# Attention's denominators gathered from SBUF to SBUF on ScalarE's queue, with their VectorE steps placed behind the newest subtraction

## The chip, the core and the metric

The kernel runs on one core of a Trainium2 chip. A core has five engines, each of which works through its own list of instructions in order: TensorE (PE in the profile) multiplies matrices, VectorE (DVE), ScalarE (ACT) and GpSimd (POOL) work element by element, and SyncE (SP) here only issues transfers. TensorE adds up its products in PSUM banks, the other tiles lie in SBUF, inputs and results in DRAM, and transfers (DMA) move data between them. An instruction that needs another engine's result waits on a semaphore, and everything behind it in its engine's list waits too. The metric is the device time of one execution in microseconds (us), smaller being better.

## The reference

Three blocks follow each other, all in fp32:

```
# attention: q, k, v are (4 batches, 8 heads, 576 tokens, 64), w_phi is (64, 128)
phi(x) = [exp(p - m), exp(-(p - m))],  p = x @ w_phi,  m = max |p| over the 128 features
kv  = sum over s of phi(k)[s, f] * v[s, d];   z = sum over s of phi(k)[s, f]
x   = (phi(q) @ kv) / (phi(q) @ z + 1e-6)            # -> 2304 tokens x 512
# ELU block: w_in (512, 2048), w_out (2048, 512)
x1  = elu(x @ w_in) @ w_out
# four experts: w1 (512, 1024), w2 (1024, 512), p = probs normalised per token
out = sum over e of p[:, e] * (relu(x1 @ w1[e]) @ w2[e])
```

## The kernel before

The work is written as Python generators; a scheduler that follows a simulated timeline then fixes each engine's list when the program is built. What was written earlier has the higher priority, and an instruction that looks ready in that timeline may be placed ahead of earlier ones that do not.

**Attention** runs over 16 pairs of heads, four to a batch, called p0 to p15 here. `pair(i)` is one generator. It projects K and Q with `w_phi` on TensorE (`md` holds the last 64 tokens of both, L205; K and Q are L188). VectorE takes the largest magnitude of each token and subtracts it (`guard`, L194 and L195), which gives `md`, `kp0`, `kp1`, `qd0` and `qd1`. ScalarE takes the exponentials of K (L198, L199). TensorE transposes Q (L234, L272), multiplies K's features with V (L227, L228) and forms the numerators (`num`, L307). V carries a column of ones, so that each head's denominator falls out as one row of its 128-row result. ScalarE copies the results to `nd0` and `nd1` (L309), 128 partitions by 576 tokens each.

The **denominators' path** is the end of `pair`. SyncE writes the two denominator rows to DRAM (`dscr`, L316), reads them back as a tile of 128 partitions by 9 (`dn`, L319), VectorE adds 1e-6 and takes the reciprocal (L321, L322), SyncE writes that to DRAM (`rscr`, L323) and reads it back broadcast over 64 partitions a head (`rb`, L327), and VectorE multiplies `nd` by it into `xf` (L331, two halves). `put_x` splits `xf` into `xh` and `xl` (ScalarE L291, GpSimd L294) and stores it.

`attention()` keeps about three pairs going: a new one starts every five rounds, and a round advances each pair by one `yield`. So while pair i is at its products, pair i+1 is in the middle and pair i+2 at its K projection.

**The ELU block** runs over nine tiles of 256 tokens and four units each. `l1` multiplies `x` by `w_in` in three products (L493 to L495), `g` is made by ScalarE (L501, L502) and VectorE (L504), split into `gh` and `gl`, and `l2` multiplies by `w_out` (L522 to L524). Between matmuls it calls `slot()`, which advances attention and the weights a little. A tile of 256 tokens needs all four pairs of its batch, so the tiles that start a new batch are written behind as many attention steps as that takes.

**The weights** of this block come as 64-bit words and are converted in 64 pieces (`convert64`): a load (L103), two ScalarE operations (L111, L112), four VectorE operations on `pcs`, `top` and `w` (L114 to L117), and two to three GpSimd and ScalarE operations. `weight_stream` keeps `CVB` = 4 of them going.

**After attention** come the upper half of the ELU block (L613 to L615, L692 to L694) and the experts (L613 to L615, L715 to L717).

SyncE's list holds the loads of K, Q, V and weights and the denominators' transfers of all pairs, in one order.

Of the kernel before, what the change touches and what calls it, by code (L numbers as in the profile page):

```python
# [8 lines left out]
F32 = mybir.dt.float32  # L9
F32R = mybir.dt.float32r  # L10
U32 = mybir.dt.uint32
I64 = mybir.dt.int64
ACTF = mybir.ActivationFunctionType
ALU = mybir.AluOpType
# [3 lines left out]
B, H, S, D, FEAT = 4, 8, 576, 64, 128  # L18
NT, DM, DFF, E, F2 = 2304, 512, 2048, 4, 1024
P = 128  # L20
KD = DM // P
NP = H // 2
# [22 lines left out]
RATE = 1.4  # L45
WRATE = 2
CVB = 4
TAIL = 2
ATE = 6
WSLOW = 2.5  # L50
# [7 lines left out]
CVW = 256  # L58
# [6 lines left out]
def attn_elu_moe_kernel(ctx: ExitStack, tc: tile.TileContext, kq_in, vv, w_phi, w_in, w_out, probs, w1, w2, out):  # L65
    nc = tc.nc
    V, A, G, PE, SP = nc.vector, nc.scalar, nc.gpsimd, nc.tensor, nc.sync
# [9 lines left out]
    dram = ctx.enter_context(tc.tile_pool(name="dram", bufs=1, space=bass.MemoryType.DRAM))  # L77
# [2 lines left out]
    x1fin = [[dram.tile([P, KD, TC], F32, name=f"x1fin{g}_{s}") for s in range(2)] for g in range(NG)]  # L80
    yscr = [dram.tile([P, DM], F32, name=f"yscr{r}") for r in range(NT // P)]
    xvd = [[dram.tile([P, 2, 2, TC], F32, name=f"xvd{g}_{k}") for k in range(7)] for g in range(NG)]
    dscr, rscr = ([dram.tile([2, S], F32, name=f"{n}{i}") for i in range(B * NP)] for n in ("den", "rec"))
    x1scr = [dram.tile([P, KD, TS], F32, name=f"x1scr{t}") for t in range(NTS)]
    ring = pool("ring", RING)
    pst = ExitStack()
# [4 lines left out]
    cv = pool("cv", CVB, stack=right, side="right")  # L91
# [7 lines left out]
        V.tensor_tensor(out=pr, in0=pr, in1=prr.to_broadcast([P, NT // P, E]), op=ALU.mult)  # L99

    def convert64(dst, src, adder):
        st = cv.tile([P, CVW], I64, tag="w64", name="w64")
        SP.dma_start(st, src)  # L103
        yield
        words = st.bitcast(U32).rearrange("p (n two) -> p n two", two=2)
        lo, hi = words[:, :, 0], words[:, :, 1]
        top = cv.tile([P, CVW], U32, tag="top", name="top")
        unit[0] += 1
        ps = pcs[:, unit[0] % 2]
        bits = ps.bitcast(U32)  # L110
        A.activation(ps, f32(hi), ACTF.Abs)  # L111
        A.activation(f32(lo), lo, ACTF.Copy, scale=2.0 ** -52)  # L112
        yield
        V.tensor_scalar(out=ps, in0=ps, scalar1=MINF, scalar2=MAXF, op0=ALU.max, op1=ALU.min)  # L114
        V.tensor_scalar(out=bits, in0=bits, scalar1=3, scalar2=0x3FFFFFF8, op0=ALU.logical_shift_left, op1=ALU.bitwise_and)
        V.scalar_tensor_tensor(out=top, in0=hi, scalar=0xC0000000, in1=bits, op0=ALU.bitwise_and, op1=ALU.bitwise_or)
        V.tensor_scalar(out=hi, in0=top, scalar1=0xFF800000, scalar2=None, op0=ALU.bitwise_and)  # L117
        yield
        G.tensor_tensor(out=f32(lo), in0=f32(lo), in1=f32(hi), op=ALU.mult)
        yield  # L120
        adder.tensor_tensor(out=f32(top), in0=f32(top), in1=f32(lo), op=ALU.add)
        if dst.dtype == F32:
            yield
            SP.dma_start(dst, f32(top))
            return
        A.activation(dst[:, 0], f32(top), ACTF.Copy)
        yield
        G.tensor_tensor(out=dst[:, 1], in0=f32(top), in1=f32(dst[:, 0]), op=ALU.subtract)
# [6 lines left out]
    a1 = pool("a1", stack=att)  # L135
# [35 lines left out]
    loaded = {0: load(0)}  # L171

    def blocks(t, n):
        return t[:, :n * P].rearrange("p (n f) -> p n f", f=P)

    def pair(i):
        b, p = divmod(i, NP)
        kq, v = loaded.pop(i)
# [12 lines left out]
        def guard(dst, ps, n):  # L191
            src = blocks(ps, n)
            mx = a1.tile([P, n, 1], F32, tag=f"mx{n}", name="mx", bufs=2)
            V.tensor_reduce(out=mx[:, :, 0], in_=src, op=ALU.max, axis=AX.X, apply_absolute_value=True)  # L194
            V.tensor_tensor(out=dst, in0=src, in1=mx.to_broadcast([P, n, P]), op=ALU.subtract)  # L195

        def kexp(d0, d1, src):
            A.activation(d0, src, ACTF.Exp)  # L198
# [84 lines left out]
        xf = a1.tile([P, S], F32, tag="xf", name="xf")  # L283
# [10 lines left out]
                G.tensor_tensor(out=xl[:, p, c:c + n], in0=xf[:, o:o + n], in1=f32(xh[:, p, c:c + n]), op=ALU.subtract)  # L294
                o += n

        nd = [a1.tile([P, S], F32, tag=f"nd{h}", name=f"nd{h}") for h in range(2)]

        def num(s):
            sl = slice(s * HS, (s + 1) * HS)  # L300
# [10 lines left out]
        num(0)  # L311
        yield
        num(1)
        yield
        for h in range(2):
            SP.dma_start(dscr[i][h:h + 1, :], nd[h][D - h * D:D - h * D + 1, :])  # L316
        yield
        dn = a1.tile([P, S // D], F32, tag="dn", name="dn")
        SP.dma_start(dn, dscr[i].rearrange("h (a b) -> (h a) b", b=S // D))  # L319
        yield  # L320
        V.tensor_scalar(out=dn, in0=dn, scalar1=1e-6, scalar2=None, op0=ALU.add)  # L321
        V.reciprocal(out=dn, in_=dn)  # L322
        SP.dma_start(rscr[i].rearrange("h (a b) -> (h a) b", b=S // D), dn)  # L323
        yield
        rb = a1.tile([P, S], F32, tag="rb", name="rb")
# [2 lines left out]
        yield  # L328
        for h in range(2):
            r = slice(h * D, h * D + D)  # L330
            V.tensor_tensor(out=xf[r], in0=nd[h][r], in1=rb[r], op=ALU.mult)  # L331
        put_x()

    done = [0]
# [69 lines left out]

    def weight_stream():
        todo = conversions()
        live = []
        more = True
        while more or live:
            if more and len(live) < CVB:  # L410
                g = next(todo, "end")
                if g == "end":
                    more = False
                else:
                    live.append(g)
            for _ in range(2):
                for g in list(live):
                    with tc.high_priority(offset=CVOFF):
                        ended = next(g[0], "end") == "end"
                    if ended:  # L420
                        live.remove(g)
                        nm, f, o = g[1]
                        if nm == "out" and f % 2 and o + CVW == 512:
                            ready.add(("elu", f // 2))
                    yield
            if not live:
                yield
        while wst[0] is None:
            yield
        for e in range(-1, E):  # L430
            for q in range(NQ):
                st = []
# [48 lines left out]
    class Elu:  # L481
# [4 lines left out]
        def l1(self, slot):  # L486
            xh, xl = xt[self.t]
            ph = bank((P, 2, TS))
            for j in range(2):
                w = rings["in", 2 * self.u + j]  # L490
                for kc in range(KD):
                    c = slice(kc * P, (kc + 1) * P)
                    PE.matmul(ph[:, j], w[:, 0, c], xh[:, kc], start=(kc == 0), stop=False)  # L493
                    PE.matmul(ph[:, j], w[:, 0, c], xl[:, kc], start=False, stop=False)  # L494
                    PE.matmul(ph[:, j], w[:, 1, c], xh[:, kc], start=False, stop=(kc == KD - 1))  # L495
                if j == 0:
                    slot()
            g = tmp.tile([P, 2, TS], F32, tag="g", name="g")
            self.gh = gt.tile([P, 2, TS], F32R, tag="gh", name="gh")
            self.gl = gt.tile([P, 2, TS], F32R, tag="gl", name="gl")  # L500
            A.activation(g, ph, ACTF.Relu, scale=-1.0)  # L501
            A.activation(g, g, ACTF.Exp, scale=-1.0)  # L502
            slot()
            V.scalar_tensor_tensor(out=g, in0=g, scalar=1.0, in1=ph, op0=ALU.subtract, op1=ALU.max)  # L504
            A.activation(self.gh, g, ACTF.Copy)  # L505
            (V if self.t >= GLV else G).tensor_tensor(out=self.gl, in0=g, in1=f32(self.gh), op=ALU.subtract)  # L506
            if self.t == NTS - 1:
                release(("in", 2 * self.u), ("in", 2 * self.u + 1))
# [458 lines left out]
```

## Time and profile before

| | us |
|---|---|
| median of 3 runs | 1439.79 |
| lowest, highest | 1436.64, 1442.32 |
| the profiled execution's own time | 1437.25 |
| its span, first to last instruction | 1435.2 |

| engine | busy us | share of the span |
|---|---|---|
| TensorE, matmuls | 1376.3 | 96% |
| VectorE | 690.8 | 48% |
| ScalarE | 630.4 | 44% |
| GpSimd | 418.5 | 29% |

The mean granted TensorE clock is 0.983, where 1 is 2.4 GHz and 0.5 is 1.2 GHz. The shares are means over stages that differ: up to about 400 us attention shares the engines with the ELU block, and from about 500 us on TensorE hardly pauses. In a table by stretches the columns are the stretch, its length, the busy time of PE, PEld, DVE, ACT and POOL with the number of instructions, the granted clock, the DMA engines' share and GB/s. In a timeline they are start, duration, engine, line, operation and tiles, and in brackets the idle time of that engine just before and what ended it. A table of waits gives, for each pair of waiting and awaited instruction, the total, the number of times and the longest, in us.

### The profile page before, as it was taken

The numbers are of one execution on the slowest core, as the hardware profiler recorded it, in microseconds if no ns is written. First come the engines' busy times: TensorE is split into PE (matmuls) and PEld (weight loads), VectorE is DVE, ScalarE is ACT, GpSimd is POOL, SyncE is SP. The second block draws the span as 40 slices with busy tenths as digits, with TensorE's granted clock in tenths as the row PEclk, the third lists the DMA queues.
The fourth block names the chain that finished last, engine by engine and source line by source line (L and its number), as shares of the span: only waits on it lengthen the run. The fifth ranks groups of instructions, "written<-read, shape, count | busy, mean of one in ns | idle before, by whom it ended". The sixth has DMA issues, their size and how long they took to land.

```text
span 1435.2 us, 21878 instructions
## 1 busy us (share of the span) xinstructions
PE 1376.3 (96%) x8224; PEld 1269.6 (88%) x8224; DVE 690.8 (48%) x1233; ACT 630.4 (44%) x1417; POOL 418.5 (29%) x487
## 2 busy tenths in 40 slices
PE   6789989999999899999999999999999999999998
PEld 5678879899989899999988988898988989889897
DVE  7767677544365384776334333233432335323232
ACT  5667667555545664574333433122431214322121
POOL 5547676533324420254212341001330004300000
PEclk9889989999999999999999999999999999999999
DMA  5443555322041412336433323524154361433421
GB/s 163 131 139 109 171 161 163 106 86 60 33 132 52 133 61 73 115 127 232 150 132 121 118 78 118 199 90 154 45 161 173 97 209 50 139 110 133 167 75 66
DMA packets 105594, 173.53 MB, mean 121 GB/s; under 512 B 33264, under 2 KB 50800, under 8 KB 105488
## 3 DMA queue, kind: packets, MB, share of 16 engines
q1 hardware_dynamic: 100592, 162.70, 35.0%
q10 hardware_dynamic: 4896, 9.44, 1.8%
q8 instruction: 64, 1.05, 0.3%
q14 instruction: 42, 0.34, 0.1%
HBM read 118.21 MB, written 53.89 MB: 120 GB/s over the span
## 4 chain that ended last, share of the span: by engine, by line
PE 71%; DMA 6%; DVE 3%; issue 2%; ACT 1%; POOL 1%; SPq 0%; DVEq 0%; POOLq 0%; ACTq 0%
PE bank L615 9%; PE bank L613 9%; PE bank L614 9%; PE bank L715 9%; PE bank L716 9%; PE bank L717 9%; PE bank L692 2%; PE bank L693 2%; PE bank L694 2%; PE bank L523 1%; PE bank L522 1%; PE bank L307 1%; PE bank L524 1%; PE bank L493 1%; PE bank L494 1%
## 5 line engine op out<-in xcount | busy, mean ns | idle before, releaser
L614 PE MATMUL bank<-xv,w 128*128 128x384 f32 x840 | 282.0, 336 | 0.0
L613 PE MATMUL bank<-xv,w 128*128 128x384 f32 x840 | 278.5, 336 | 3.0 <-DVE c L664 2.2
L615 PE MATMUL bank<-xv,w 128*128 128x384 f32 x840 | 277.9, 336 | 0.0
L715 PE MATMUL bank<-w,h 128*128 128x512 f32 x576 | 225.8, 395 | 2.6 <-ACT h L629 2.6
L716 PE MATMUL bank<-w,h 128*128 128x512 f32 x576 | 227.4, 395 | 0.0
L717 PE MATMUL bank<-w,h 128*128 128x512 f32 x576 | 202.9, 396 | 0.0
L455 POOL TENSOR_TENSOR w<-wst,w 128x256 fp32r<-128x256 f32 x100 | 78.1, 800 | 363.1 <-ACT w L454 348.0
L613 PEld LDWEIGHTS bank<-xv,w 128*128 128x128 f32 x840 | 157.8, 188 | 11.3 <-DVE c L664 2.5
L614 PEld LDWEIGHTS bank<-xv,w 128*128 128x128 f32 x840 | 157.8, 188 | 4.8
L615 PEld LDWEIGHTS bank<-xv,w 128*128 128x128 f32 x840 | 157.5, 188 | 0.0
L630 DVE SCALAR_TENSOR_TENSOR h<-bank,h 128x384 fp32r<-128x384 f32 x144 | 77.1, 554 | 125.5 <-ACT h L629 125.4
L629 ACT ACTIVATE h<-bank 128x384 fp32r<-128x384 f32 x144 | 66.8, 489 | 152.4 <-PE bank L615 94.7
L715 PEld LDWEIGHTS bank<-w,h 128*128 128x128 f32 x576 | 108.2, 188 | 25.6 <-ACT h L629 3.6
L716 PEld LDWEIGHTS bank<-w,h 128*128 128x128 f32 x576 | 108.3, 188 | 23.0
L717 PEld LDWEIGHTS bank<-w,h 128*128 128x128 f32 x576 | 107.2, 188 | 21.9 <-DVE h L630 1.1
L619 ACT ACTIVATE cmab<-bank 128x384 f32<-128x384 f32 x60 | 29.4, 491 | 192.3 <-PE bank L615 192.3
L564 POOL TENSOR_TENSOR xv<-xs,xv 128x768 fp32r<-128x768 f32 x24 | 46.7, 1950 | 191.2 <-ACT xv L563 182.5
L493 PE MATMUL bank<-xh,w 128*128 128x256 f32 x288 | 85.0, 295 | 0.4 <-DVE g L504 0.2
L523 PE MATMUL bank<-gl,w 128*128 128x256 f32 x288 | 81.8, 286 | 3.0 <-DVE gl L506 2.5
L627 DVE TENSOR_TENSOR c<-cmab,bank 128x384 f32<-128x384 f32 x48 | 26.6, 554 | 120.1 <-ACT cmab L619 120.1
L522 PE MATMUL bank<-gh,w 128*128 128x256 f32 x288 | 81.2, 292 | 3.0 <-ACT gh L505 3.0
L494 PE MATMUL bank<-xl,w 128*128 128x256 f32 x288 | 81.9, 284 | 0.0
(117 smaller groups left out, 2803.4 us busy)
## 6 DMA issues: line engine op xcount, KB each, us to landing
xv<-xvd SPq DMA_DIRECT2D x42, 768.0 KB
wst<-in_w SPq DMA_DIRECT2D x64, 256.0 KB
xvd<-xv SPq DMA_DIRECT2D x21, 768.0 KB
yscr<-y SPq DMA_DIRECT2D x54, 256.0 KB
y<-yscr SPq DMA_DIRECT2D x54, 256.0 KB
w<-in_w_in SPq DMA_DIRECT2D x32, 256.0 KB
w<-in_w_out SPq DMA_DIRECT2D x32, 256.0 KB
kq<-in_kq SPq DMA_DIRECT2D x16, 320.0 KB
```

The lines of the kernel that those rows point to most:

```text
L455: on[WL[v % len(WL)]].tensor_tensor(out=lo, in0=x, in1=f32(hi), op=ALU.subtract)
L493: PE.matmul(ph[:, j], w[:, 0, c], xh[:, kc], start=(kc == 0), stop=False)
L494: PE.matmul(ph[:, j], w[:, 0, c], xl[:, kc], start=False, stop=False)
L522: PE.matmul(o, w[:, 0, c], self.gh[:, j], start=start, stop=False)
L523: PE.matmul(o, w[:, 0, c], self.gl[:, j], start=False, stop=False)
L613: PE.matmul(o, hi[:, c], x[:, 0, kc], start=not more and kc == 0, stop=False, skip_group_check=more)
L614: PE.matmul(o, hi[:, c], x[:, 1, kc], start=False, stop=False, skip_group_check=more)
L615: PE.matmul(o, lo[:, c], x[:, 0, kc], start=False, stop=kc == 1, skip_group_check=more)
L630: V.scalar_tensor_tensor(out=h[:, 1], in0=c, scalar=0.0, in1=f32(h[:, 0]), op0=ALU.max, op1=ALU.subtract)
L715: PE.matmul(self.acc, h[:, 0, c], w[:, 0], start=f == 0, stop=False)
L716: PE.matmul(self.acc, h[:, 0, c], w[:, 1], start=False, stop=False)
L717: PE.matmul(self.acc, h[:, 1, c], w[:, 0], start=False, stop=f == 2 * NQ - 1)
```

## The change

It has four parts.

1. `dn` is filled directly from the denominator rows in `nd0` and `nd1`, by two transfers from SBUF to SBUF (L319 of the new kernel, 64 partitions by 9 each), issued by ScalarE. The DRAM tile `dscr`, its three transfers per pair on SyncE and two `yield`s per pair are gone.
2. The steps of VectorE on the denominators (add, reciprocal, and the two products into `xf`) may not be placed ahead of the newest subtraction written so far: `mark` holds the last L195 or L504 instruction, and `tc.issue_after` adds an edge of order, without a semaphore.
3. `nd0` and `nd1` have two buffers each.
4. `weight_stream` keeps `CVL` = 2 further pieces loaded, whose load has been issued and whose conversion has not begun.

```
-        nd = [a1.tile([P, S], F32, tag=f"nd{h}", name=f"nd{h}") for h in range(2)]
+        nd = [a1.tile([P, S], F32, tag=f"nd{h}", name=f"nd{h}", bufs=2) for h in range(2)]
...
         num(1)
-        yield
-        for h in range(2):
-            SP.dma_start(dscr[i][h:h + 1, :], nd[h][D - h * D:D - h * D + 1, :])
-        yield
         dn = a1.tile([P, S // D], F32, tag="dn", name="dn")
-        SP.dma_start(dn, dscr[i].rearrange("h (a b) -> (h a) b", b=S // D))
-        yield
-        V.tensor_scalar(out=dn, in0=dn, scalar1=1e-6, scalar2=None, op0=ALU.add)
-        V.reciprocal(out=dn, in_=dn)
+        for h in range(2):
+            A.dma_start(dn[h * D:h * D + D], nd[h][D - h * D:D - h * D + 1, :].rearrange("o (a b) -> o a b", b=S // D))
+        yield
+        with tc.issue_after(mark[0]):
+            V.tensor_scalar(out=dn, in0=dn, scalar1=1e-6, scalar2=None, op0=ALU.add)
+            V.reciprocal(out=dn, in_=dn)
...
-            V.tensor_tensor(out=xf[r], in0=nd[h][r], in1=rb[r], op=ALU.mult)
+            with tc.issue_after(mark[0]):
+                V.tensor_tensor(out=xf[r], in0=nd[h][r], in1=rb[r], op=ALU.mult)
...
-        while more or live:
-            if more and len(live) < CVB:
+        while more or loaded or live:
+            if more and len(loaded) < CVL:
                 g = next(todo, "end")
...
-                    live.append(g)
+                    next(g[0])
+                    loaded.append(g)
+            if loaded and len(live) < CVB and (len(loaded) == CVL or not more):
+                live.append(loaded.pop(0))
```

`mark[0]` is set where `guard` subtracts and where L504 of the old kernel computes `g`.

The lists of the engines, first VectorE's in the first batch. The names end in a number of their own; `nd0_585` and `nd0_595` belong to p1, and `kp0_694` and `kp0_700` are K's subtraction of p3. Before:

```order
L115 TENSOR_SCALAR pcs_175<-pcs_175 128x256
L116 SCALAR_TENSOR_TENSOR top_784<-w64_777,pcs_175 128x256
L331 TENSOR_TENSOR xf_584<-nd0_585,rb_780 64x576
L117 TENSOR_SCALAR w64_777<-top_784 128x256
L194 TENSOR_REDUCE mx_753<-bank_743 128x4
L331 TENSOR_TENSOR xf_584<-nd1_586,rb_780 64x576
L194 TENSOR_REDUCE mx_774<-bank_744 128x4
L114 TENSOR_SCALAR pcs_175<-pcs_175 128x256
L195 TENSOR_TENSOR kp0_694<-bank_743,mx_753 128x4x128
L195 TENSOR_TENSOR kp1_695<-bank_744,mx_774 128x4x128
```

And now:

```order
L118 TENSOR_SCALAR w64_697<-top_764 128x256
L197 TENSOR_REDUCE mx_761<-bank_751 128x4
L197 TENSOR_REDUCE mx_787<-bank_752 128x4
L115 TENSOR_SCALAR pcs_159<-pcs_159 128x256
L198 TENSOR_TENSOR kp0_700<-bank_751,mx_761 128x4x128
L333 TENSOR_TENSOR xf_594<-nd0_595,rb_714 64x576
L333 TENSOR_TENSOR xf_594<-nd1_596,rb_714 64x576
L198 TENSOR_TENSOR kp1_701<-bank_752,mx_787 128x4x128
```

The products of p1 stood ahead of both maxima of p3's K; they now stand behind both maxima and the first subtraction, and still ahead of the second.

The second place is again VectorE's list, in the stage where attention and the ELU block share the engines, around the products of p6 (`nd0_1919` before, `nd0_1913` now). Before:

```order
L321 TENSOR_SCALAR dn_2110<-dn_2110 128x9
L322 RECIPROCAL dn_2110<-dn_2110 128x9
L114 TENSOR_SCALAR pcs_175<-pcs_175 128x256
L194 TENSOR_REDUCE mx_2087<-bank_2085 128x2
L115 TENSOR_SCALAR pcs_175<-pcs_175 128x256
L116 SCALAR_TENSOR_TENSOR top_2549<-w64_2332,pcs_175 128x256
L117 TENSOR_SCALAR w64_2332<-top_2549 128x256
L331 TENSOR_TENSOR xf_1918<-nd0_1919,rb_2247 64x576
L114 TENSOR_SCALAR pcs_175<-pcs_175 128x256
L504 SCALAR_TENSOR_TENSOR g_2105<-g_2105,bank_2042 128x512
L331 TENSOR_TENSOR xf_1918<-nd1_1920,rb_2247 64x576
L195 TENSOR_TENSOR md_2082<-bank_2085,mx_2087 128x256
```

And now:

```order
L198 TENSOR_TENSOR md_2074<-bank_2077,mx_2079 128x256
L118 TENSOR_SCALAR w64_2502<-top_2617 128x256
L115 TENSOR_SCALAR pcs_159<-pcs_159 128x256
L116 TENSOR_SCALAR pcs_159<-pcs_159 128x256
L117 SCALAR_TENSOR_TENSOR top_2697<-w64_2592,pcs_159 128x256
L282 TENSOR_TENSOR kvl_2051<-bank_2047,kvh_2050 128x512
L118 TENSOR_SCALAR w64_2592<-top_2697 128x256
L197 TENSOR_REDUCE mx_2189<-bank_2179 128x4
L197 TENSOR_REDUCE mx_2226<-bank_2180 128x4
L115 TENSOR_SCALAR pcs_159<-pcs_159 128x256
L198 TENSOR_TENSOR kp0_2072<-bank_2179,mx_2189 128x4x128
L333 TENSOR_TENSOR xf_1912<-nd0_1913,rb_2106 64x576
```

The product stood ahead of `g`, of p8's `md` subtraction and of `kvl`; it now stands behind `md`, `kvl` and `kp0` of the same pair p8.

The third place is SyncE's list at p1's denominators, before:

```order
L143 DMA kq<-in_kq 128x640
L146 DMA kq<-in_kq 128x512
L316 DMA den_126<-nd_585 1x576
L316 DMA den_126<-nd_586 1x576
L319 DMA dn<-den_126 128x9
L148 DMA vt_200<-in_vv 128x4x64
L150 DMA vt_200<-in_vv 64x64
L103 DMA w_829<-in_w_out 128x256
L323 DMA rec_142<-dn 128x9
L103 DMA w_864<-in_w_out 128x256
L327 DMA rb<-rec_142 64x576 x2
```

And now:

```order
L144 DMA kq<-in_kq 128x640
L147 DMA kq<-in_kq 128x512
L324 DMA rec_126<-dn 128x9
L149 DMA vt_184<-in_vv 128x4x64
L151 DMA vt_184<-in_vv 64x64
L328 DMA rb<-rec_126 64x576 x2
L104 DMA w_836<-in_w_in 128x256
L104 DMA w_863<-in_w_in 128x256
```

The three transfers that filled `dn` have left the list, and the next weight loads (`w_836`, `w_863`) stand behind the broadcast `rb` where `w_829` and `w_864` stood ahead of it.

## Rows read from the trace of the kernel before

**Rows 1.** Busy time by stretch of the span; columns as told above.

```profile
31.00:104.30 73.30, 58.66 (x401) 50.66 (x401) 49.95 (x111) 44.15 (x122) 36.78 (x56) 0.86 0.46 132
104.30:275.00 170.70, 155.64 (x1230) 146.93 (x1229) 128.63 (x277) 115.57 (x285) 117.26 (x152) 0.95 0.48 146
```

**Rows 2.** Timeline of PE in the first batch.

```profile
31.14 0.30 PE L234 MATMUL bank<-ident,qd 128*128 128x128 f32 x1 [0.73 <-DVE qd L195]
...
37.31 1.16 PE L188 MATMUL bank<-wbd,kq 64*128 64x128 f32 x16
...
48.51 0.45 PE L234 MATMUL bank<-ident,qd 128*128 128x128 f32 x1 [3.80 <-ACT kp L199]
...
68.77 0.45 PE L234 MATMUL bank<-ident,qd 128*128 128x128 f32 x1 [4.35 <-DVE qd L195]
...
77.52 1.16 PE L188 MATMUL bank<-wbd,kq 64*128 64x128 f32 x16
...
88.73 0.45 PE L234 MATMUL bank<-ident,qd 128*128 128x128 f32 x1 [4.28 <-ACT nd L309]
```

**Rows 3.** Timeline of DVE, 91 to 109 us.

```profile
95.02 0.20 DVE L322 RECIPROCAL dn<-dn 128x9 f32<-128x9 f32 x1
...
100.19 1.01 DVE L331 TENSOR_TENSOR xf<-nd,rb 64x576 f32<-64x576 f32 x1 [1.49 <-DMA rb<-rec]
101.12 0.40 DVE L116 SCALAR_TENSOR_TENSOR top<-w,pcs 128x256 uint32<-128x256 uint32 x1
101.56 0.76 DVE L331 TENSOR_TENSOR xf<-nd,rb 64x576 f32<-64x576 f32 x1
102.34 1.29 DVE L194 TENSOR_REDUCE mx<-bank 128x4 f32<-128x512 f32 x2
...
107.71 1.27 DVE L195 TENSOR_TENSOR qd<-bank,mx 128x512 f32<-128x512 f32 x2
```

**Rows 4.** Timeline of SP, 60 to 80 us.

```profile
68.20 0.86 SPq L316 DMA_DIRECT2D den<-nd  x2
69.97 0.34 SPq L319 DMA_DIRECT2D dn<-den  x1
```

**Rows 5.** Waits of PE, 112 to 410 us.

```profile
PE bank L188 <- DVE md L195: 4.2, 3, 2.7
PE bank L188 <- DVE g L504: 3.4, 2, 3.2
PE bank L307 <- ACT eh L252: 2.2, 1, 2.2
PE bank L307 <- DVE g L504: 1.7, 1, 1.7
PE bank L523 <- DVE gl L506: 1.5, 2, 0.8
...
PE bank L188 <- DVE kvl L279: 1.1, 1, 1.1
```

**Rows 6.** Waits of DVE, 112 to 410 us.

```profile
DVE xf L331 <- DMA rb<-rec: 27.3, 12, 4.8
DVE dn L321 <- DMA dn<-den: 26.8, 11, 4.7
```

**Rows 7.** The chain that ended last, 300 to 335 us.

```profile
321.45 1.92 DMA den<-nd
323.39 1.78 DMA dn<-den
...
325.64 1.42 DMA rec<-dn
...
327.57 4.21 DMA rb<-rec
```

**Rows 8.** Groups of ACT by line, 25 to 112 us.

```profile
L112 ACT ACTIVATE w<-w 128x256 f32<-128x256 uint32 x19 | 8.3, 439 | 4.9 <-DMA w<-in_w_in 3.0 <-DMA w<-in_w_out 1.9
```

**Rows 9.** Waits of SP over the whole span.

```profile
SPq L316 <- ACT nd L309: 61.8, 25, 19.2
```

More of the change, by code (lines that the diff above doesn't have):

```diff
@@ L47 @@
 CVB = 4
+CVL = 2
 TAIL = 2
@@ L82, in attn_elu_moe_kernel @@
     xvd = [[dram.tile([P, 2, 2, TC], F32, name=f"xvd{g}_{k}") for k in range(7)] for g in range(NG)]
-    dscr, rscr = ([dram.tile([2, S], F32, name=f"{n}{i}") for i in range(B * NP)] for n in ("den", "rec"))
+    rscr = [dram.tile([2, S], F32, name=f"rec{i}") for i in range(B * NP)]
     x1scr = [dram.tile([P, KD, TS], F32, name=f"x1scr{t}") for t in range(NTS)]
@@ L101, in convert64 @@
     def convert64(dst, src, adder):
-        st = cv.tile([P, CVW], I64, tag="w64", name="w64")
+        st = cv.tile([P, CVW], I64, tag="w64", name="w64", bufs=CVB + CVL)
         SP.dma_start(st, src)
@@ L174, in blocks @@
         return t[:, :n * P].rearrange("p (n f) -> p n f", f=P)
+    mark = [None]
     def pair(i):
@@ L194, in guard @@
             V.tensor_reduce(out=mx[:, :, 0], in_=src, op=ALU.max, axis=AX.X, apply_absolute_value=True)
-            V.tensor_tensor(out=dst, in0=src, in1=mx.to_broadcast([P, n, P]), op=ALU.subtract)
+            mark[0] = V.tensor_tensor(out=dst, in0=src, in1=mx.to_broadcast([P, n, P]), op=ALU.subtract).ins
         def kexp(d0, d1, src):
@@ L313, in pair @@
         num(1)
+        dn = a1.tile([P, S // D], F32, tag="dn", name="dn")
+        for h in range(2):
+            A.dma_start(dn[h * D:h * D + D], nd[h][D - h * D:D - h * D + 1, :].rearrange("o (a b) -> o a b", b=S // D))
         yield
-        for h in range(2):
-            SP.dma_start(dscr[i][h:h + 1, :], nd[h][D - h * D:D - h * D + 1, :])
-        yield
-        dn = a1.tile([P, S // D], F32, tag="dn", name="dn")
-        SP.dma_start(dn, dscr[i].rearrange("h (a b) -> (h a) b", b=S // D))
-        yield
-        V.tensor_scalar(out=dn, in0=dn, scalar1=1e-6, scalar2=None, op0=ALU.add)
-        V.reciprocal(out=dn, in_=dn)
+        with tc.issue_after(mark[0]):
+            V.tensor_scalar(out=dn, in0=dn, scalar1=1e-6, scalar2=None, op0=ALU.add)
+            V.reciprocal(out=dn, in_=dn)
         SP.dma_start(rscr[i].rearrange("h (a b) -> (h a) b", b=S // D), dn)
@@ L406, in weight_stream @@
         todo = conversions()
-        live = []
+        live, loaded = [], []
         more = True
-        while more or live:
-            if more and len(live) < CVB:
+        while more or loaded or live:
+            if more and len(loaded) < CVL:
                 g = next(todo, "end")
@@ L503, in l1 @@
             slot()
-            V.scalar_tensor_tensor(out=g, in0=g, scalar=1.0, in1=ph, op0=ALU.subtract, op1=ALU.max)
+            mark[0] = V.scalar_tensor_tensor(out=g, in0=g, scalar=1.0, in1=ph, op0=ALU.subtract, op1=ALU.max).ins
             A.activation(self.gh, g, ACTF.Copy)
```

## The prediction

> **What bounds the kernel now.** I read the table by stretches first. Behind 275 us TensorE pauses little; what can be won lies before. From 31 to 104.3 us, where attention works on the first batch alone, it is busy 58.66 of 73.3 us at a mean granted clock of 0.86, and from 104.3 to 275 us, where attention and the ELU block share the engines, 155.64 of 170.7 us at 0.95 [rows 1]. That is 14.6 and 15.1 us idle. Low clock comes on top: at most (1 - 0.95) x 170.7 = 8.5 us in the second stage, and in the first I take it from the timeline below.
>
> Next TensorE's timeline in the first batch. Each pair is a block that starts with a transpose, and the starts lie at 31.14, 48.51, 68.77 and 88.73: periods of 17.4, 20.3 and 20.0 us [rows 2]. Before the last three starts TensorE is idle for 3.80, 4.35 and 4.28 us. It then pays twice: from the start of the block to the K projection takes 37.31 - 31.14 = 6.2 us behind a pause of 0.73 us and 77.52 - 68.77 = 8.75 us behind one of 4.35 us [rows 2]. The extra 2.6 us are matmuls at the lower clock level (1.2 GHz).
>
> Why a block starts late is read on VectorE. The reciprocal ran at 95.02 us, 6.3 us into the block, since it stood behind `md`'s maximum, which waited for TensorE. The product into `xf` could not start until `rb` landed, at 100.19. Behind it stood both maxima of K, at 102.34, and the subtractions of Q, at 107.71 [rows 2, 3]. K's projection had long been ready. So the period is a ring: reciprocal, two transfers (5.2 us), the products, VectorE's chain, and TensorE again.
>
> In the shared stage the same two waits stand on VectorE: 27.3 us for `rb` and 26.8 us for `dn` [rows 6]. TensorE's waits there are mostly for what is queued behind them: `md`, `g`, `eh`, `gl` and `kvl`, 4.2 + 3.4 + 2.2 + 1.7 + 1.5 + 1.1 = 14.1 us [rows 5].
>
> **The change part by part.**
>
> *The first batch.* Now the products of pair i stand behind the maxima and the first subtraction of pair i+2, and `dn` behind the subtractions of Q of pair i+1. Take a block that starts at 0. ScalarE had the denominator rows ready when SyncE began to issue at 68.20, 0.6 us before the block at 68.77 [rows 2, 4]. Two issues cost 0.86 us there. A transfer of the kind now used does not stand in the trace; the nearest are `den` and `dn` at 1.92 and 1.78 us [rows 7]. I bound it by 1.4 (`rec`, the shortest of that chain) and 4.2 us (`rb`, the longest), and take 1.8, since `dn` moves the same pieces into the same tile. So `dn` lands about 2.0 us into the block, and the reciprocal, with a conversion or two between, ends near 2.7 instead of 6.3. Add the 5.2 us from the reciprocal to the product: `rb` is there at 7.9 us.
>
> When is it wanted? K's projection ends 6.2 + 1.16 = 7.3 us into the block at full clock, 9.9 at the lower one [rows 2]. The two maxima (1.29), a conversion step (0.40) and one subtraction (half of 1.27) bring VectorE to 9.6 us or later. `rb` is 1.7 us early, so the wait on the product goes. What is late next is VectorE's own chain: the two products (2 x 0.76), the second subtraction (0.64), two conversion steps (0.8), Q's maxima (1.29), its first subtraction (0.64). In all 7.2 us from the K projection to the next start, by durations of [rows 3]. The period is 7.3 + 7.2 = 14.5 us, or 17.1 if the clock still falls.
>
> Against the three periods (17.4, 20.3, 20.0) and the last part block, which has only its clock to win, that saves 2.9 + 5.8 + 5.5 + 2.6 = 16.8 us, or 0.3 + 3.2 + 2.9 = 6.4. In the first case TensorE's pause shrinks to about 1 us, close to the 0.73 us behind which the clock held, so I start from 16.8. One thing is taken off: the next weight loads now stand behind `rb` in SyncE's list, and ScalarE's first conversion step stands ahead of its exponentials. ScalarE already waited 4.9 us for weight loads in this stage [rows 8]; I let all of it come onto the path. That leaves 12 us.
>
> *The shared stage.* The products stand behind `md`, `kvl` and `kp0` instead of ahead of `md`, `g` and `kvl`, which are what TensorE waited for. The bound above is 14.1 us of waits plus 8.5 us of clock, 22.6; the bound below is 0, if something else on VectorE or ScalarE is late in each place. I take half, 11 us, because `dn`'s wait is only shortened by one transfer (1.92 of the 3.70 us of `den` and `dn`, [rows 7]) and what follows it still waits.
>
> *Issues on ScalarE.* 32 issues at 0.43 us [rows 4] are 13.8 us. They lie behind the copies of `nd` and beside an engine that is busy 44 of 73 and 116 of 171 us [rows 1]; I charge 1 us, at most 13.8 if each stands before an exponential that TensorE awaits.
>
> *Two buffers for `nd`, weights loaded ahead, 48 issues fewer on SyncE.* Nothing in the sum. What hides them is that TensorE waits for none of them in [rows 5]; at most they give back the 4.9 us above, and if they cost, it is the same 4.9.
>
> At the queues I weigh a page against the trace. SyncE's list stood 61.8 us, in 25 waits, for `nd` [rows 9], with loads behind it. The Trainium skill ("DMA: Bandwidth & Descriptors", Issuing engines are not separate DMA queues) says that transfers from different engines share the same 16 DMA engines, so that issuing from another one saves only the time of the issue, which is usually small. By it moving the issues is worth nothing beside the trip that is dropped, and the sum stays at 20.5. By the row the freed list could bring loads forward and the 4.9 us back, for a sum of 25.4.
>
> *Products queued later.* `xf` now waits for a whole further K projection. Where an ELU tile needs the last pair of a batch, TensorE may meet it: 1.5 us.
>
> Sum: 12 + 11 - 1 - 1.5 = 20.5 us. Against the profiled execution's 1437.25 us that is 1416.75. The median of the runs is 2.5 us above that execution, so I say 1419.
>
> **The rivals.**
>
> *All of it is won.* The clock holds in every block, no weight load comes late, and each wait of [rows 5] goes: 16.8 + 22.6 = 39.4 us, 1437.25 - 39.4 + 2.5 = 1400. For it: all named waits sit behind the two transfers. Against it: VectorE is busy 128.6 of 170.7 us in the shared stage [rows 1], and an engine that full makes others wait.
>
> *The waits come back one step on.* `dn` stands right behind Q's subtractions, the weight loads stand behind `rb`, and the clock falls after each pause as before. Then only 6.4 us of the first batch are won and nothing in the shared stage; with 1 us for the issues it is 1437.25 - 5.4 + 2.5 = 1434. For it: the lists are placed close to what a simulated timeline expects of transfers, and [rows 6] shows both waits in nearly every pair, so that the placement was too early each time. Against it: `rb`'s place moved back by more than its wait.
>
> *Slower: the last pair's `x` comes late.* At tiles 0, 2, 4 and 6 the ELU block needs the batch's last pair, whose products now stand behind a K subtraction two pairs on. TensorE works in order, so a matmul that lacks `x` stops all. The price is the longest wait for `rb` seen, 4.8 us [rows 6], and the 2.6 us of low clock behind such a pause: 7.4 us a place, 29.6 for four. It decides from two places on, if of the rest only the 6.4 us are won: 1437.25 + 14.8 - 5.4 + 2.5 = 1449; with four, 1464. For it: the edge is one of order, and it holds when VectorE has nothing else to do. Against it: ELU matmuls of earlier units can fill the gap.
>
> **How the numbers follow.** The forecast has 0.65, the full gain 0.15, the waits that come back 0.13, the late `x` 0.07. Within 0.5% of 1439.79, 7.2 us either way, a measurement of this kernel can't be told from no change. Faster is the first two, 0.80; the same 0.13; slower 0.07. The range reaches from the full gain, 1400, to 1438, just past the rival in which the waits come back; the forecast's own bounds (6.4 to 16.8, 0 to 22.6) lie inside it.
>
> **What would show it.** Right: block starts in the first batch 15 to 17 us apart, the first ELU matmul 8 to 14 us earlier than 104.3, the wait of the product for `rb` below 5 us in all where it was 27.3 in the shared stage, and a granted clock above 0.93 in the first batch. Wrong in the first term: periods still near 20 with VectorE or ScalarE waiting for a weight load or for `dn`. Wrong in the second: TensorE's waits in the shared stage above 10 us, with new names. Wrong as a whole: a TensorE wait for `xh` or `xl` of several us at the start of tile 2, 4 or 6.

## The result, and the profile after

The changed kernel takes 1423.18 us in the median of 4 runs (1421.24 to 1425.21), against 1440.28 us in 4 runs of the kernel before. The ratio, here and below worked out from the single runs and so not always the quotient of two medians, is 0.9884, with a 95% interval of 0.9858 to 0.991: 1.2% faster. The forecast was 1419 us in a range of 1400 to 1438. The profiled executions differ by 12.5 us (spans of 1435.2 and 1422.7). The rest of the 17.1 us between the medians is spread of runs: the profiled execution of before lies 3.0 us below its median, that of after 1.3 us above.

Busy time by stretch in the kernel after (stretch, length, busy time of PE, PEld, DVE, ACT and POOL with their counts, granted clock, DMA share, GB/s):

```profile
31.00:104.30 73.30, 60.84 (x451) 52.35 (x449) 58.61 (x130) 50.76 (x138) 43.50 (x65) 0.95 0.52 151
104.30:275.00 170.70, 162.45 (x1275) 154.77 (x1276) 124.44 (x265) 114.76 (x282) 112.08 (x146) 0.96 0.49 144
```

Against [rows 1] TensorE idles 12.5 us instead of 14.6 in the first stretch and 8.3 instead of 15.1 in the second. The clock in the first is 0.95, where it was 0.86.

TensorE's timeline in the kernel after (start, duration, engine, line, operation; in brackets the idle time just before and what ended it). L237, L191 and L310 are the old L234, L188 and L307, and L498 is the old L493:

```profile
32.17 0.30 PE L237 MATMUL bank<-ident,qd 128*128 128x128 f32 x1 [0.60 <-DVE qd L198]
...
48.10 0.45 PE L237 MATMUL bank<-ident,qd 128*128 128x128 f32 x1 [3.05 <-DVE qd L198]
...
65.18 0.45 PE L237 MATMUL bank<-ident,qd 128*128 128x128 f32 x1 [2.96 <-DVE qd L198]
...
72.70 1.16 PE L191 MATMUL bank<-wbd,kq 64*128 64x128 f32 x16
...
81.86 0.30 PE L237 MATMUL bank<-ident,qd 128*128 128x128 f32 x1 [1.48 <-DVE qd L198]
...
89.13 0.39 PE L498 MATMUL bank<-xh,w 128*128 128x256 f32 x1
...
106.63 0.80 PE L527 MATMUL bank<-gh,w 128*128 128x256 f32 x2 [3.91 <-ACT gh L510]
...
379.04 0.29 PE L310 MATMUL bank<-eh,kvl 128*128 128x288 f32 x1
```

The blocks start 15.9, 17.1 and 16.7 us apart, where [rows 2] has 17.4, 20.3 and 20.0. The pauses ahead of them are shorter but not gone. The first ELU matmul comes at 89.13 instead of 104.28 us. A wait of 3.91 us for `gh` from ScalarE stands behind it; the kernel before waits twice for `gh`, 1.9 us in all.

VectorE's waits over the whole span of the kernel after (us in total, times, longest):

```profile
DVE dn L322 <- DMA dn<-nd: 22.3, 13, 4.7
DVE xf L333 <- DMA rb<-rec: 4.5, 3, 2.6
```

The wait for `rb` is all but gone; between 112 and 410 us alone it was 27.3 [rows 6]. The wait for `dn` is not: between 112 and 410 us it fell from 26.8 [rows 6] to 19.5 us, although the new path has one transfer less.

A lead can be read off the last numerators of attention, which are at this row of TensorE's timeline in the kernel before:

```profile
389.95 0.30 PE L307 MATMUL bank<-eh,kvl 128*128 128x288 f32 x1
```

At the fourth block start the new kernel leads by 88.73 - 81.86 = 6.9 us, at the last numerators by 389.95 - 379.04 = 10.9, at the end by 12.5. So 6.9 us come from the first batch, 4.0 from the shared stage and 1.6 from what follows.

### The profile page after: what moved, and what is told of

It reads as the page before. It is cut to its first block, busy times and chain, and to the rows that moved or that the text cites. A ratio compares the mean times of both kernels' runs of the same rounds, so it can differ in the third digit from the quotient of the medians.

```text
span 1422.7 us, 21849 instructions
## 1 busy us (share of the span) xinstructions
PE 1376.4 (97%) x8224; PEld 1270.9 (89%) x8224; DVE 689.6 (48%) x1233; ACT 628.9 (44%) x1417; POOL 415.5 (29%) x487
## 4 chain that ended last, share of the span: by engine, by line
PE 77%; DMA 4%; issue 3%; DVE 2%; POOL 2%; ACT 1%; SPq 0%; ACTq 0%; DVEq 0%; POOLq 0%
PE bank L618 10%; PE bank L620 10%; PE bank L619 10%; PE bank L720 9%; PE bank L722 9%; PE bank L721 9%; PE bank L697 2%; PE bank L698 2%; PE bank L699 2%; PE bank L528 2%; PE bank L527 2%; PE bank L529 2%; PE bank L230 2%; PE bank L498 2%; PE bank L191 1%
## 5 line engine op out<-in xcount | busy, mean ns | idle before, releaser
L498 PE MATMUL bank<-xh,w 128*128 128x256 f32 x288 | 84.1, 293 | 1.3 <-DVE g L509 0.9
L632 DVE TENSOR_TENSOR bank<-cm,bank 128x384 f32<-128x384 f32 x48 | 26.9, 561 | 116.1 <-PE bank L620 101.0
```

## The experiments

Each ratio is to the kernel before on the same chip, with its 95% interval. "The edge" is the order edge of part 2, and a lead is read as above, from the profiled executions.

**The edge alone** (before, with parts 2 and 3).

```
+            with tc.issue_after(mark[0]):
+                V.tensor_tensor(out=xf[r], in0=nd[h][r], in1=rb[r], op=ALU.mult)
```

> The kernel before with only the order edge on VectorE's denominator steps and two buffers for nd; denominators still go through DRAM on SyncE. Theory 1 (VectorE no longer stands for rb ahead of what TensorE needs): most of the gain, 1425 to 1431 us, and VectorE's wait of the product for rb below 10 us over the span where it was 35.5. Theory 2 (the dropped trip and the freed SyncE list make the gain): 1436 us or more.

Measured: 1417.74 us, 0.9876 (0.9858 to 0.9894), faster than the range expected. The waits for `rb` and `dn` are 8.6 and 3.9 us over the span. With the denominators still going through DRAM, this is all that the full change gave. Part 3 was not run apart from the edge.

**The path alone** (before, with part 1).

```
-            SP.dma_start(dscr[i][h:h + 1, :], nd[h][D - h * D:D - h * D + 1, :])
+            A.dma_start(dn[h * D:h * D + D], nd[h][...].rearrange("o (a b) -> o a b", b=S // D))
```

> The kernel before with only the denominators moved from SBUF to SBUF on ScalarE's queue (and two yields fewer per pair). Theory 1: a small gain, 1432 to 1439 us, with the wait of the product for rb still above 20 us over the span. Theory 2: 1422 to 1428 us.

Measured: 1432.14 us, 0.999 (0.9972 to 1.0009): no change. Over the span the wait for `dn` falls from 29.2 to 17.2 us and the one for `rb` rises from 35.5 to 42.9.

**The change without the edge.**

```
-        with tc.issue_after(mark[0]):
-            V.tensor_scalar(out=dn, in0=dn, scalar1=1e-6, scalar2=None, op0=ALU.add)
...
-            with tc.issue_after(mark[0]):
-                V.tensor_tensor(out=xf[r], in0=nd[h][r], in1=rb[r], op=ALU.mult)
+            V.tensor_tensor(out=xf[r], in0=nd[h][r], in1=rb[r], op=ALU.mult)
```

> The changed kernel without the order edge, all else kept. Theory 1: 1431 to 1439 us, waits for rb back above 20 us. Theory 2: 1421 to 1427 us, as the changed kernel.

Measured: 1427.72 us, 0.9966 (0.9944 to 0.9987), between the two ranges expected, with twelve runs from 1424.53 to 1438.62. The profiled execution, one of the longer (1437.88), has 43.5 us of waits for `rb`. Parts 1, 3 and 4 together are worth 0.1 to 0.6%; the edge brings the rest.

**The change without part 4.**

```
-            if more and len(loaded) < CVL:
+            if more and len(live) < CVB:
...
-                    next(g[0])
-                    loaded.append(g)
+                    live.append(g)
```

> The changed kernel without the two pieces loaded ahead. Theory 1: 1420 to 1427 us, no difference that can be measured. Theory 3 (weights loaded ahead keep ScalarE and VectorE from waiting): 1430 us or more, and ScalarE's waits of L112 and L113 for weight loads above 15 us between 25 and 92 us where the changed kernel has 9.1.

Measured: 1421.51 us, 0.9899 (0.9881 to 0.9917). ScalarE waits 10.0 us for weight loads between 25 and 104 us, and 11.2 with part 4. Loading two pieces ahead does nothing that can be measured.

**The edge on the two products only** (before, with two buffers for `nd`; the steps on `dn` stay free).

```
-            V.tensor_tensor(out=xf[r], in0=nd[h][r], in1=rb[r], op=ALU.mult)
+            with tc.issue_after(mark[0]):
+                V.tensor_tensor(out=xf[r], in0=nd[h][r], in1=rb[r], op=ALU.mult)
```

> The kernel before with two buffers for nd and the order edge on the products into xf alone, not on the add and the reciprocal. Theory 1 (the products' place is what counts): 1416 to 1422 us, within 0.3% of the version with both edges (1417.74), waits for rb below 12 us over the span. Theory 1b (the place of the add and reciprocal counts as much): 1425 us or more.

Measured: 1417.94 us, 0.9873 (0.9855 to 0.989). The wait for `rb` falls to 1.6 us, that for `dn` to 14.7. The products' place is what the change earned its time with. It waits 10.8 us longer for `dn` than the edge alone, 7.0 less for `rb`, and takes the same time.

**The new transfers issued by SyncE.**

```
-            A.dma_start(dn[h * D:h * D + D], nd[h][...])
+            SP.dma_start(dn[h * D:h * D + D], nd[h][...])
```

> The changed kernel with the two SBUF to SBUF transfers issued by SyncE. Theory 1 (the queue counts little): ratio to the kernel before within 0.004 of the changed kernel's 0.988. Theory 2 (a freed SyncE list gives the gain): ratio 0.994 or more, with ScalarE's waits for weight loads between 25 and 104 us above 15 us where the changed kernel has 11.2.

Measured: 1419.6 us, 0.9889 (0.9872 to 0.9907). The queue of issue makes no difference that can be measured.

**Half as many steps of the weight stream in the first batch.** `PRE` is how many of its steps are taken for each step of attention until the first batch is done.

```
-PRE = 2
+PRE = 1
```

> The changed kernel with one weight step per attention step instead of two before the first ELU matmul (half as many pieces in the first batch). Theory A (the weight pieces between VectorE's attention steps, and their loads that ScalarE waits for, keep the first batch's period at 16 to 17 us): periods of 14 to 15.5 us there, the fourth block's start 4 us or more before 81.86; the whole 0 to 6 us faster, as the pieces are owed later. Theory B (the pieces lie beside other work): periods stay at 16 to 17 us.

Measured: 1421.0 us, 0.9892 (0.9873 to 0.9911), with periods of 16.1, 17.6 and 16.5 us. It does not tell the theories apart, since the conversions did not become fewer in the first batch: ScalarE's first step on a piece (L113) runs 20 times between 25 and 104 us in either kernel, and ScalarE still waits 12.2 us for weight loads there.

**The two empty yields put back**, ahead of the transfers.

```
         num(1)
+        yield
+        yield
         dn = a1.tile([P, S // D], F32, tag="dn", name="dn")
```

> The changed kernel with two empty yields per pair put back, so that attention advances against the ELU block as before. Theory 1: the pace counts little, ratio to the kernel before within 0.004 of 0.988. Theory 4 (a share of the gain comes from fewer steps per pair): ratio 0.993 or more, with TensorE's idle time between 104 and 275 us back above 12 us where the changed kernel has 8.2.

Measured: 1424.84 us, 0.992 (0.9905 to 0.9935). The waits are 3.3 us for `dn` and 10.4 for `rb`, yet it is not faster than the change. TensorE idles 14.5 us from 104.3 to 275 us, above the 12 that theory 4 named, where the change has 8.3. Attention runs two rounds longer per pair; that these cost the time is not shown apart from the steps' place.

After these eight, two theories stood for what was left: VectorE standing at `dn`, and ScalarE standing at weight loads.

**One more yield between the transfers and the steps on `dn`.**

```
             A.dma_start(dn[h * D:h * D + D], nd[h][...])
         yield
+        yield
         with tc.issue_after(mark[0]):
```

> The changed kernel with one more yield between the transfers into dn and VectorE's steps on it, so that the mark is one subtraction later: add and reciprocal stand behind md's subtraction of the next pair instead of behind Q's. Theory A: what is left of the first batch's period (16.6 us against 15.4 of the order edge alone) is VectorE standing at dn, 22.3 us over the span, for a transfer that ScalarE issues at 64.87 and 65.69 and VectorE wants at 66.9. Then the wait for dn falls below 6 us, the block starts come 15 to 16 us apart, and the ratio to the kernel before is 0.983 to 0.986. Theory B: ScalarE's wait for weight loads (11 us in that stretch) sets the period. Then the starts stay 16 to 17 us apart with the wait for dn gone, and the ratio stays 0.987 to 0.990. Theory C: one more round for every pair costs pace, as the two empty yields did: 0.990 to 0.993.

Measured: 1406.94 us, 0.9792 (0.9774 to 0.981). That is 2.1% faster than before, and beyond what theory A hoped for. `md`'s subtraction now stands ahead of `dn`, and both of K's ahead of the products. VectorE's waits over the span and its timeline there (L323 is the add):

```profile
DVE xf L334 <- DMA rb<-rec: 5.3, 3, 3.6
DVE dn L323 <- DMA dn<-nd: 2.7, 1, 2.7
```

```profile
70.62 0.42 DVE L198 TENSOR_TENSOR md<-bank,mx 128x256 f32<-128x256 f32 x1
70.95 0.16 DVE L323 TENSOR_SCALAR dn<-dn 128x9 f32<-128x9 f32 x1
```

`dn` is there when it is wanted. Where the time came from is seen in the stretches and on TensorE's timeline of this kernel:

```profile
31.00:104.30 73.30, 64.80 (x475) 56.95 (x474) 59.00 (x132) 50.80 (x137) 43.86 (x67) 0.93 0.50 152
104.30:275.00 170.70, 163.44 (x1361) 155.31 (x1360) 128.54 (x273) 120.13 (x301) 116.44 (x151) 0.99 0.47 146
```

```profile
81.40 0.30 PE L237 MATMUL bank<-ident,qd 128*128 128x128 f32 x1 [1.95 <-DVE qd L198]
...
364.14 0.29 PE L310 MATMUL bank<-eh,kvl 128*128 128x288 f32 x1
```

The fourth block starts within half a microsecond of the change's, so the first batch gained next to nothing and theory A was wrong on its periods (15.3, 17.2 and 16.7 us). The lead over before grows from 7.3 us there to 25.8 at the last numerators: 18.5 us in the shared stage, where the change won 4.0. In the second stretch its clock is 0.99 against 0.96, and 1361 matmul instructions are counted against 1275.

**The weight loads issued by GpSimd.**

```
-        SP.dma_start(st, src)
+        G.dma_start(st, src)
```

> The changed kernel with the weight loads of the conversion issued by GpSimd instead of SyncE, so that they no longer stand in SyncE's list behind the transfers rec and rb, which wait for VectorE. Theory B: ScalarE's wait for weight loads is late because its loads stand there; then it falls from 11.2 us to below 5 us between 25 and 104 us, the block starts come 15 to 16 us apart, and the ratio is 0.982 to 0.986. Theory A: the wait for dn sets the period; then the ratio stays 0.987 to 0.990, and the starts 16 to 17 us apart. Rival D: GpSimd, which multiplies and subtracts for the same conversions, issues the loads no earlier, since it stands at its own waits (31 us in that stretch); then ScalarE's wait stays above 8 us and the ratio is 0.988 to 0.995.

Measured: 1420.63 us, 0.9874 (0.9853 to 0.9896). ScalarE's wait for weight loads falls from 11.2 to 5.9 us between 25 and 104 us; VectorE's for `dn` stays at 20.5 over the span. The periods are 15.7, 16.0 and 16.9 us, and the time does not move. The fourth block starts at 78.64 us, 3.2 ahead of the change's, 2.1 of them ahead at the first; at the last numerators (379.97 us) this lead is gone. So either this half of ScalarE's wait was not on the path, or GpSimd's added work (busy 54.5 us instead of 43.5 from 31 to 104.3) took as much back.

The last two ask whether the path or the place made the 2.1%.

**The edge, the path through DRAM, and one yield less** (the edge alone, without the yield ahead of the `den` transfers).

```
-        yield
         for h in range(2):
             SP.dma_start(dscr[i][h:h + 1, :], nd[h][D - h * D:D - h * D + 1, :])
```

> The kernel before with the order edge on dn's steps and on the products, two buffers for nd, and one yield less between the numerators and dn's steps; the denominators still go through DRAM on SyncE's queue, and the weights are loaded as before. VectorE's list in the first batch is then that of the changed kernel with one more yield: dn behind md's subtraction, the products behind both of K's. Theory A: the place of dn and of the products in VectorE's list is the whole gain, and the trip through DRAM is hidden. Then the ratio to the kernel before is 0.977 to 0.982, as with the transfer from SBUF to SBUF (0.979), and the wait for dn stays below 6 us. Theory B: that place can only be met by the shorter path. Then dn is waited for 10 us or more in the span and the ratio is 0.984 to 0.990.

Measured: 1406.48 us, 0.98 (0.978 to 0.9819). VectorE's waits over the span and TensorE's last numerators:

```profile
DVE xf L334 <- DMA rb<-rec: 5.4, 3, 3.0
DVE dn L323 <- DMA dn<-den: 3.4, 2, 3.0
```

```profile
359.11 0.29 PE L309 MATMUL bank<-eh,kvl 128*128 128x288 f32 x1
```

With the same place in VectorE's list, the trip through DRAM and the one from SBUF to SBUF give the same time. (This kernel and the edge alone also lack part 4, which by itself measured nothing.)

**Two more yields there, with the new path.**

```
             A.dma_start(dn[h * D:h * D + D], nd[h][...])
         yield
+        yield
+        yield
         with tc.issue_after(mark[0]):
```

> The changed kernel with two more yields between the transfers into dn and VectorE's steps on it: the steps stand behind K's first subtraction, the products behind Q's, as in the kernel before with the order edge alone (0.988). Theory A: the place and the pace set the time, not the path. Then the ratio is 0.985 to 0.991, and both waits on VectorE are below 9 us together. Theory B: the path counts, and what one more yield won (0.979 against 0.988) comes from the shorter path with the waits gone. Then the ratio is 0.976 to 0.982.

Measured: 1419.93 us, 0.9892 (0.9872 to 0.9912). The waits are 3.3 us for `dn` and 8.6 for `rb`. Together they are above the 9 us expected, and 3 to 4 above those of the two fastest kernels. The time is again that of the edge alone, which has as many yields. TensorE's longest wait between 92 and 400 us is now of another kind, and its last numerators come late:

```profile
PE bank L310 <- ACT eh L255: 6.2, 1, 6.2
```

```profile
376.16 0.29 PE L310 MATMUL bank<-eh,kvl 128*128 128x288 f32 x1
```

Side by side, by yields between the numerators and the steps on `dn` (all with the edge):

| yields | through DRAM | SBUF to SBUF |
|---|---|---|
| 1 | not run | 0.9884 (the change) |
| 2 | 0.98 | 0.9792 |
| 3 | 0.9876 | 0.9892; 0.992 with two of them ahead of the transfers |

The path changes nothing that can be measured in either row that has both. The number of yields does, and the best is in the middle.

## Why the prediction was right, and where its terms were off

The direction and the main cause came out, but the sum was too large. The forecast's ratio to its own median, 1419 to 1439.79 or 0.9856, lies just below the measured interval, and of the 20.5 us summed up the profiled executions show 12.5. The medians come nearer, 17.1 us apart, partly because the profiled execution of before lies below its median; that part is luck.

**Products queued later: right.** The mechanism is the one forecast. Queued behind K's maxima and first subtraction, the products find `rb` landed: 4.5 us of wait in the whole span, below the 5 us named. The edge on the products alone gives the whole gain, and no kernel without the edge gets below 0.9944 at the low end of its interval. `x` did not come late: TensorE's wait for `xh` is 0.5 us between 112 and 410 us. Of the rival in which the waits come back one step on, two conditions showed in part, `dn`'s wait (19.5 of 26.8 us left) and the weight loads, but the wait did not return at `rb`, and the time was 11 us below the 1434 it gave. The signs named came out too: blocks 15.9 to 17.1 us apart, a clock of 0.95 in the first batch, and the first ELU matmul 15.2 us earlier, just past the 8 to 14.

**First batch: right in kind, its parts off.** The three periods were to give 14.2 us less 4.9 for weights, 9.3. They gave 57.59 - 49.69 = 7.9 us, and the first block started 1.0 us later. Three steps of the working were off. The first is the landing of `dn`, which was to come 2.0 us into the block. VectorE's timeline of the kernel after shows it at 3.5:

```profile
66.45 0.43 DVE L116 TENSOR_SCALAR pcs<-pcs 128x256 uint32<-128x256 uint32 x1
68.66 0.17 DVE L322 TENSOR_SCALAR dn<-dn 128x9 f32<-128x9 f32 x1 [1.78 <-DMA dn<-nd]
69.11 0.21 DVE L323 RECIPROCAL dn<-dn 128x9 f32<-128x9 f32 x1
...
72.76 0.43 DVE L115 TENSOR_SCALAR pcs<-pcs 128x256 f32<-128x256 f32 x1 [0.95 <-ACT pcs L112]
...
74.97 1.28 DVE L197 TENSOR_REDUCE mx<-bank 128x4 f32<-128x512 f32 x2
76.17 0.68 DVE L198 TENSOR_TENSOR kp<-bank,mx 128x512 f32<-128x512 f32 x1
76.77 1.75 DVE L333 TENSOR_TENSOR xf<-nd,rb 64x576 f32<-64x576 f32 x2
```

ScalarE's timeline of the same kernel shows why (ACTq is its issuing of transfers):

```profile
64.87 0.47 ACTq L319 DMA_DIRECT2D dn<-nd  x1
65.25 0.40 ACT L312 ACTIVATE nd<-bank 128x288 f32<-128x288 f32 x1
65.55 0.41 ACT L112 ACTIVATE pcs<-w 128x256 f32<-128x256 f32 x1
65.69 0.47 ACTq L319 DMA_DIRECT2D dn<-nd  x1
```

The second issue stands behind its own copy of `nd`, and ends at 66.16, 1.0 us after the block start at 65.18. Then the transfer takes its time, as the view of the tile `dn` in the same kernel says of all 32:

```profile
L319 ACTq DMA_DIRECT2D dn<-nd x32: 471/472/607, 32.9 to 380.0; - x32
...
DMA to landing us min/median/max: 1.4/1.9/5.2
```

The first row has the duration of an issue in ns. I had taken 1.8 us for the landing, close to the median of 1.9, but `dn` is whole only when the later of two has landed. The reciprocal ended 4.1 us into the block instead of 2.7. The products (76.77) still waited for nothing, so no row shows that this lengthened the period.

The second step is VectorE's chain. It was to take 7.2 us from the end of the K projection to the next block. That projection ended at 72.70 + 1.16 = 73.86, the next block began at 81.86: 8.0 us. A conversion that had waited for ScalarE (72.76) stood ahead of the maxima, which began at 74.97.

The third is the clock, and in this block it weighs most. I had let TensorE's pause shrink to about 1 us and the block run at full clock. The pauses were 3.05, 2.96 and 1.48 us, and behind the second one K's projection began 72.70 - 65.18 = 7.5 us into the block instead of 6.2. The granted clock of that stretch (the figure behind the brackets) is 0.80:

```profile
65.18:72.70 7.52, 7.52 (x52) 7.30 (x53) 4.43 (x14) 4.19 (x12) 4.08 (x7) 0.80 0.18 47
```

So this period of 16.7 us lies near the lower-clock end of my two, 14.5 and 17.1: about 1.3 of the 2.2 us above 14.5 lie ahead of the K projection, at the lower clock, and 0.8 in VectorE's chain.

**Weight loads: on the path they cost less than charged.** ScalarE's wait for them rose as feared: these rows of its waits between 25 and 104 us make 11.2 us, where [rows 8] had 4.9 in a slightly longer stretch.

```profile
ACT w L113 <- DMA w<-in_w_out: 5.7, 6, 2.7
ACT w L113 <- DMA w<-in_w_in: 5.5, 6, 1.3
```

But taking 5.3 us of it away, with GpSimd as issuer, did not move the whole time. So the 4.9 us that I charged for them brought the sum nearer to the measured one, but no run shows that they are the reason.

**The shared stage: the step that failed, by size.** I took 11 us, half of TensorE's waits and lost clock, and with the last part block (2.6), the issues (-1) and the later products (-1.5) the forecast had 11.1 us from the fourth block start on. Measured are 4.0 + 1.6 = 5.6. One more round ahead of the steps on `dn` won 18.5 us in this stage, so the upper bound of 22.6 us was near what is to be had.

The reason given for halving was that `dn`'s wait is only shortened, and it was, from 26.8 to 19.5 us. That this wait is what the stage lost is not shown. It is 2.7 us over the span in the kernel with one more yield, but only 3.3 to 3.9 in three others (the edge alone, the two yields put back, two more yields). Their waits for `dn` and `rb` together are 12 to 14 us, where the change has 26.8, and none of them is measurably faster than the change.

The sign I had named for this failure, more than 10 us of TensorE's waits under new names, did show if the stage is counted from its first ELU matmul. From 89 to 410 us TensorE's waits in the change add up to 12.3 us, where the kernel before has 17.4 from 104 us on. These are the longest:

```profile
PE bank L527 <- ACT gh L510: 4.2, 2, 3.9
PE bank L528 <- POOL gl L511: 2.2, 2, 2.0
PE bank L310 <- ACT kvw L279: 1.6, 1, 1.6
```

In the stretch of [rows 5], from 112 us on, they are only 6.8.

One place where the change lost time can be cut out, since it holds the same ELU matmuls in both kernels (16 of each of the three `l1` lines and two of `l2`). It lies between these starts of `md`'s projection on TensorE's timeline, in the change and then in the kernel with one more yield:

```profile
84.29 0.60 PE L208 MATMUL bank<-wbd,kq 128*128 128x256 f32 x2
...
112.34 0.68 PE L208 MATMUL bank<-wbd,kq 128*128 128x256 f32 x2
```

```profile
85.36 0.71 PE L208 MATMUL bank<-wbd,kq 128*128 128x256 f32 x2
...
107.31 0.50 PE L528 MATMUL bank<-gh,w 128*128 128x256 f32 x2 [0.77 <-ACT gh L511]
...
107.66 0.59 PE L208 MATMUL bank<-wbd,kq 128*128 128x256 f32 x2
```

These are 28.0 and 22.3 us, in the change and with one more yield, and the granted clock is 0.88 and 1.00:

```profile
84.29:112.34 28.05, 22.55 (x155) 20.39 (x154) 21.40 (x46) 18.84 (x48) 18.26 (x27) 0.88 0.38 110
```

```profile
85.36:107.66 22.30, 21.21 (x173) 19.51 (x173) 17.27 (x39) 15.82 (x42) 13.40 (x21) 1.00 0.53 157
```

In the change TensorE waits 3.91 us for `gh`; with one more yield it waits 0.77. No step on `dn` stands ahead of that `gh` in VectorE's rows from 95 us on. ScalarE's timeline in the change, then TensorE's, and TensorE's with one more yield show what does:

```profile
102.58 0.58 ACT L506 ACTIVATE g<-bank 128x512 f32<-128x512 f32 x1
104.25 0.43 ACT L113 ACTIVATE w<-w 128x256 f32<-128x256 uint32 x1 [1.08 <-DMA w<-in_w_out]
104.58 0.61 ACT L507 ACTIVATE g<-g 128x512 f32<-128x512 f32 x1
```

```profile
107.23 1.05 PE L237 MATMUL bank<-ident,qd 128*128 128x128 f32 x4
```

```profile
101.70 0.60 PE L237 MATMUL bank<-ident,qd 128*128 128x128 f32 x4
```

A weight load that comes late holds up the second step of `g`; VectorE's step on `g` follows at 105.23 us, `gh` at 105.95. And the next pair's transposes, whose subtraction of Q ends at 101.4 us in the change, stand behind the matmul of `gh` there and ahead of it with one more yield, where they fill the gap. That place holds 5.7 of the 14.5 us between the two in this stage, 1.9 of them up to the end of the `l1` matmuls (102.7 and 101.9 us) and 3.8 behind it; how the other 8.8 divide was not followed.

**Issues on ScalarE and the queue: worth nothing that can be measured.** The ratio is 0.9889 with SyncE as issuer and 0.9884 with ScalarE. Putting 32 issues back on the list that had stood 61.8 us for `nd` [rows 9] cost nothing, and the freed list brought back none of the 4.9 us. The Trainium skill ("DMA: Bandwidth & Descriptors", Issuing engines are not separate DMA queues) says that moving issues saves only the time of the issue itself, usually small beside the transfer. The trace agrees: 0.9889 and 0.9884. One reading was wrong: 0.43 us is half of the 0.86 us that [rows 4] has from the start of one issue to the end of the next, with a gap between. An issue of `den` itself took 0.24 us, one of the new transfers 0.47, so the 32 new issues take about 15 us and not 13.8.

**Open.** Why two yields are faster than both one and three was not settled. Each yield moves the steps on VectorE and also lengthens a pair by a round, and no run changed one without the other. With three, the waits on VectorE are nearly gone as well, and TensorE's 6.2 us for `eh` fit the longer round, but that was not tested. What sets the 16 to 17 us of the first batch is open too: neither `dn` nor half of the weight wait did. The edge alone has less there. Its blocks start at 31.36, 46.30, 62.64 and 77.76 us, the fourth 4.1 us ahead of the change's, at a granted clock of 1.00 from 31 to 104.3 us. It differs in the path, the yields and the weight loads; leaving out part 4 did not shorten the periods (16.2, 16.6 and 17.2 us), and the other two were not told apart.

## What to carry to other kernels

When an engine works in order and a transfer is late on it, look first at what stands behind the waiting instruction: moving it back by a few instructions gained 1.2% here, while shortening the transfer path by a trip through DRAM gained nothing. Then try the places next to the new one. One round more gave another 0.9%, and the waits on that engine did not tell it beforehand: three kernels in which the wait for `dn` was nearly gone were no faster. When two changes come as one, path and place here, a table of four runs tells which of them counts.

## What the runs showed of the hardware

A small transfer from SBUF to SBUF, one row of 576 values into 64 partitions by 9, was no quicker than one of the steps through DRAM: 1.9 us in the median and 5.2 at most to land, against 1.92 and 1.78 us for `den` and `dn` [rows 7]. Its issue took 0.47 us on ScalarE (median of 32) and 0.49 on SyncE, about twice the 0.24 us of an issue of `den`, one plain row to DRAM. The view of the tile `den` in the kernel before (least, median and most, in ns) has:

```profile
L316 SPq DMA_DIRECT2D den<-nd x32: 225/242/305, 31.5 to 390.7; - x32
```
